# A fused attention and MLP kernel: the first chunk's q and k products made together, row tile by row tile, and the warm-up products fed from the program's constant zero

## The chip, the cores and the metric

The kernel runs on one core of one Trainium2 chip. The metric is device time in microseconds of one execution. Three runs of the kernel before took 414.65, 414.2 and 414.75 us; the median is 414.65. The profiled execution took 414.58 us, of which 412.7 us are the span from the first to the last instruction that the profile shows.

## The reference

For each token the result is a gated sum of an attention branch and an MLP branch, on the same input x of 2048 tokens by 448 features:

```python
g = sigmoid((x * gate_w).sum(-1, keepdims=True))
q, k, v = split(x @ wqkv)            # 16 heads of 28
# each token attends to itself and 7 earlier ones, 2 apart
logits = einsum("bhsd,bhswd->bhsw", q, k[idx]) * 28 ** -0.5   # masked where idx < 0
a = einsum("bhsw,bhswd->bhsd", softmax(logits), v[idx]) @ wo
b = relu(x @ w1 + b1) ** 2 @ w2 + b2  # 1792 hidden
out = g * a + (1 - g) * b
```

All inputs are float32. The change touches the first quarter of x @ wqkv alone.

## The kernel before

**Products in three parts.** Each float32 operand is split into a high part (rounded to the array's fp32r type by an ACT copy) and a low part (the rest, by a VectorE subtraction). A product of two operands is then three matrix products: high x high, high x low and low x high. In the names, `h` and `l` end the tiles: `wqh` and `wql` for the weights of q, k and v, `x.h` and `x.l` for the input.

**Tiling.** The 2048 tokens are four chunks of 512, each of four tiles of 128 tokens. The contraction has 448 rows: three row tiles of 128 (numbers 0 to 2) and a last one of 64, which is stored twice, on the lower and the upper 64 partitions (`w7h`, `w7l`, `x.x7`, `x.x8`). For each tile of tokens and each of q, k and v there is one PSUM accumulator (`Acc`) of 128 tokens by 448 columns (450 for q: two more columns carry the gate); it takes 3 x 3 full products and 3 on the last 64 rows. PSUM has eight accumulators, four under the tag `m` and four under `b`.

**Pairs.** TensorE can run two products on 64 rows side by side, one on the lower and one on the upper half of the array. `side_by_side` (L180) issues such pairs. A full product can also be made as two half products, one on each half, which must not be in flight on the same accumulator at once; `turn` (L191) stands between the halves: a tiny write to the accumulator by VectorE (or ACT), which waits for the first half and for which the second half waits.

**The first chunk, `qkv_first` (L257).** First, q of all four tiles (tag `b`), full products on 128 rows, row tile by row tile (L266): 12 products each, 36 in all. Then `run` works through a list of pairs: the last 64 rows of q beside those of k (12 pairs), then the 128-row products of k as half products (36 pairs), then v (42 pairs). v's four accumulators take the PSUM buffers of q.

**Evacuation, `qkv_evacuate` (L201).** ACT copies a finished accumulator to a staging tile `st` (L207) and, for q, the gate column to `zg` (L215). A staging tile holds two tiles of tokens; when the second is in, one DMA of 448 KB stores it to `q_d`, `k_d` or `v_d` (L213). There are `ST_BUFS = 3` staging buffers. In the first chunk q is evacuated as 0, 1, 2, 3, while the first pairs run, and k as 0, 2, 1, 3, later.

**The order of the work.** Nothing reorders instructions: each engine runs its own in program order, and waits by semaphores. Around the products a planner decides where in the program side work is issued. `advance` (L478) adds the planned time of the products just issued to a clock, and issues what `when` (L677) or `at` has set for an earlier time: the splits of v's weights at 12.0 us and 0.9 us apart, the spill of x to `x_d` at 10.5, the splits of the next chunk's x at 19.0 (`SPLIT_AT`, L682), the load of the chunk after at 23.5. `run` calls `advance` after each up to 12 pairs, then issues the step's turns, then its evacuations. All loads and stores go through SP's queue, one after the other.

**The start.** The program's constants are set by GpSimd ahead of a barrier (L1162). Then `WARM = 13` products of 128 x 256 on a tile of zeros (L632), which VectorE clears first (L629), keep TensorE busy until the first data is there. Meanwhile SP issues loads: for each row tile q's weights and x (L639, L644), then k's and v's weights (L649), the last 64 rows of v's (L652), and the next chunk's x (L565). The splits of q's weights and x follow (L654 to L667), and k's three after those (L711).

Of the kernel before, what the change touches and what calls it, by code (L numbers as in the profile page):

```python
# [7 lines left out]
F32 = mybir.dt.float32  # L8
F32R = mybir.dt.float32r
# [4 lines left out]
S, D, H, DH, W, F = 2048, 448, 16, 28, 8, 1792  # L14
P = 128
# [8 lines left out]
NQ = D + 2  # L24
# [7 lines left out]
MM448 = 203.0  # L32
# [15 lines left out]
LEAD = 5  # L48
DEFER = 2
ORDER = (3, 0, 1, 2)  # L50
WARM = 13
PP_BUFS = 4
ST_BUFS = 3
BT_BUFS = 8
# [3 lines left out]
def gated_mix_kernel(ctx: ExitStack, tc: tile.TileContext, xT, wqkv, w1, w2, wo, b1, b2, out):  # L58
    nc = tc.nc

    def f32(ap):
        return ap.bitcast(F32)
# [29 lines left out]
    attp = ctx.enter_context(tc.tile_pool(name="attp", bufs=1))  # L92
    smp = ctx.enter_context(tc.tile_pool(name="smp", bufs=2))
    prodp = ctx.enter_context(tc.tile_pool(name="prodp", bufs=1))
# [18 lines left out]
    def split_full(raw, hi, lo, soon=now):  # L113
        nc.scalar.activation(hi, raw, AF.Copy)
        soon(lambda: nc.vector.tensor_sub(lo, raw, f32(hi)))
# [29 lines left out]
    def ps(tag, name):  # L145
        return psum.tile([P, 512], F32, tag=tag, name=name, bufs=4)
# [6 lines left out]
    wqh = ap.tile([P, 3, NP + 2 * D], F32R, name="wqh")  # L153
    wql = ap.tile([P, 3, NP + 2 * D], F32R, name="wql")
# [10 lines left out]
    def ncols(b):  # L165
        return NQ if b == 0 else D

    def block(b):

        o = (0, NP, NP + D)[b]  # L170
        return slice(o, o + ncols(b))
# [8 lines left out]
    def side_by_side(*todo):  # L180


        assert len(todo[0]) == len(todo[1])
        for pair in zip(*todo):
            for r, (acc, a, w) in enumerate(pair):
                rows = slice(r * 64, r * 64 + 64)
                assert acc.rows in (None, r)
                nc.tensor.matmul(acc.pt[:, :acc.n], a[rows], w[rows], start=acc.todo == acc.all, stop=acc.todo == 1)  # L188
                acc.todo, acc.rows = acc.todo - 1, r

    def turn(one, two):  # L191


        for acc in (one, two) if one is not two else (one,):
            if one is two:
                nc.scalar.activation(acc.pt[0:1, 511:512], none, AF.Copy)
            else:
                nc.vector.memset(acc.pt[0:1, 511:512], 0.0)
            acc.rows = None
# [17 lines left out]
    def full(x, acc, tl, b, ks=range(3)):  # L217
        sl, n = slice(tl * P, tl * P + P), block(b)
        r = []
        for k in ks:  # L220
            r += [(acc, x.h[k][:, sl], wqh[:, k, n]), (acc, x.h[k][:, sl], wql[:, k, n]),
                  (acc, x.l[k][:, sl], wqh[:, k, n])]
        return r

    def last(x, acc, tl, b):

        sl = slice(tl * P, tl * P + P)
        n = block(1) if b == 2 else slice(0, ncols(b))
        h, l = w7h[:, n], w7l[:, n]
        return [(acc, x.x7[:, sl], h), (acc, x.x7[:, sl], l), (acc, x.x8[:, sl], h)]  # L230

    def accs(c, b, tls, tags):
        return [Acc(t, f"qkv{c}_{tl}_{b}", ncols(b)) for t, tl in zip(tags, tls)]

    def run(c, todo, steps):


        a = 0
        for e, done, *turns in steps:
            side_by_side(todo[0][a:e], todo[1][a:e])  # L240
            while a < e:
                n = min(12, e - a)
                if clock["on"] and a + n == e:

                    advance(max(n - LEAD, 0) * MM448)
                    while turns and not callable(turns[0]):
                        turn(*turns.pop(0))
                    n = min(n, LEAD)
                advance(n * MM448)
                a = min(a + 12, e)  # L250
            for t in turns:
                t() if callable(t) else turn(*t)
            for b, tl, acc in done:
                assert acc.todo == 0
                qkv_evacuate(acc.pt, c, tl, b)

    def qkv_first(x):  # L257


        four = range(4)  # L260
        q = accs(0, 0, four, "bbbb")
        for k in range(3):
            for two in ((0, 1), (2, 3)):
                for j, prods in enumerate(zip(*(full(x, q[i], i, 0, (k,)) for i in two))):
                    for acc, a, w in prods:
                        nc.tensor.matmul(acc.pt[:, :NQ], a, w, start=k == j == 0, stop=False)  # L266
            advance(12 * MM448)
        for acc in q:
            acc.todo = 3
        k = accs(0, 1, four, "mmmm")  # L270
        t = [sum((last(x, a[i], i, b) for i in four), []) for b, a in ((0, q), (1, k))]
        f = [full(x, k[i], i, 1) for i in four]
        run(0, [t[0] + f[0] + f[1] + f[2] + f[3], t[1] + f[2] + f[3] + f[0] + f[1]],
            [(3, [(0, 0, q[0])], (k[0], k[0])),
             (12, [(0, i, q[i]) for i in (1, 2, 3)], (k[1], k[1])),
             (24, [], (k[0], k[2])), (33, [], (k[1], k[3])),
             (39, [(1, 0, k[0]), (1, 2, k[2])]), (48, [(1, 1, k[1]), (1, 3, k[3])])])
        v = accs(0, 2, four, "bbbb")
        f, l = [full(x, v[i], i, 2) for i in four], [last(x, v[i], i, 2) for i in four]
        run(0, [f[0] + l[0] + f[2] + l[2] + f[1] + f[3], f[1] + l[1] + f[3] + l[3] + f[0] + f[2]],  # L280
            [(15, [], (v[0], v[1])), (24, [], (v[2], v[3])),
             (33, [(2, 0, v[0]), (2, 1, v[1])]), (42, [(2, 2, v[2]), (2, 3, v[3])])])
# [192 lines left out]
    def soon(fn):  # L475
        at(LO_DELAY, fn)

    def advance(dt):  # L478
        clock["pe"] += dt
        while due := [x for x in later if x[0] <= clock["pe"]]:  # L480
            item = min(due, key=lambda x: x[0])
            later.remove(item)
            item[1]()
        if not clock["on"]:
            clock["att"] = clock["pe"]
            return
        while clock["att"] < clock["pe"]:
            try:
                r = next(att)
            except StopIteration:  # L490
                clock["on"] = False
                return
            if r is None:
                clock["att"] = clock["pe"]
                return
            clock["att"] += r


    def raw_tile(name):
        return rawp.tile([P, 4, 512], F32, tag="raw", name=name)  # L500
# [124 lines left out]


    warm = ps("m", "warm")
    zero = prodp.tile([P, 2 * P], F32R, tag="pp", name="zero", bufs=PP_BUFS)
    nc.vector.memset(f32(zero), 0.0)  # L629
    nc.vector.memset(none, 0.0)  # L630
    for _ in range(WARM):
        nc.tensor.matmul(warm[:, :2 * P], zero[:, :P], zero, start=True, stop=True)  # L632


    raws = [raw_tile("wqraw0")]
    rx = raw_tile("xraw0")
    for k in range(4):
        if k < 3:
# [3 lines left out]
                nc.sync.dma_start(raws[0][rows, k, :NQ], wqkv[b, rows, k])  # L642
        for cols in ((slice(0, 256), slice(256, CH)) if k == 0 else (slice(0, CH),)):
            nc.sync.dma_start(rx[:, k, cols], xT[0, :, k, cols])  # L644

    for b, tag in ((1, "k"), (2, "v")):
        raw = attp.tile([P, 3, D], F32, tag=tag, name=f"wqraw{b}")
        for k in range(3):
            nc.sync.dma_start(raw[:, k], wqkv[b, :, k, :D])  # L649
        raws.append(raw)  # L650
    raw7 = attp.tile([P, D], F32, tag="q", name="wqraw7")
    nc.sync.dma_start(raw7, wqkv[2, :, 3, :D])  # L652
    x = x_tiles(0, xap)
    for k in range(3):  # L654
        nc.scalar.activation(wqh[:, k, :NQ], raws[0][:, k, :NQ], AF.Copy)
        halves = (slice(0, 256), slice(256, CH))
        for i, cols in enumerate(halves):

            if k == i == 0:
                nc.vector.tensor_copy(x.h[k][:, cols], rx[:, k, cols])  # L660
            else:
                nc.scalar.activation(x.h[k][:, cols], rx[:, k, cols], AF.Copy)
        nc.vector.tensor_sub(wql[:, k, :NQ], raws[0][:, k, :NQ], f32(wqh[:, k, :NQ]))
        for cols in halves:
            nc.vector.tensor_sub(x.l[k][:, cols], rx[:, k, cols], f32(x.h[k][:, cols]))
    split_full(raws[0][:, 3, :NQ], w7h[:, :NQ], w7l[:, :NQ])
    split_x78(rx[:, 3], x.x7, x.x8)  # L667

    def wq_split(b, k):
        if k < 3:  # L670
            split_full(raws[b][:, k], wqh[:, k, block(b)], wql[:, k, block(b)])
        else:
            split_full(raw7, w7h[:, NP:], w7l[:, NP:])
# [34 lines left out]
        nc.sync.dma_start(b1t, b1)  # L708
        nc.sync.dma_start(b2t, b2.partition_broadcast(P))

    for k in range(3):  # L711
        wq_split(1, k)
    for k in range(4):
        when(12000.0 + k * 900.0, wq_split, 2, k)
    for c, t in SPLIT_AT.items():
# [31 lines left out]
    for c in range(4):  # L747
        x = xs[c]
# [291 lines left out]
    c, x = ORDER[0], xm[3]  # L1040
# [8 lines left out]
    for g in range(2, 2 * NF):  # L1049
        i, f = g // (NF // 2), g % (NF // 2) * 2  # L1050
# [3 lines left out]
        last = g == 2 * NF - 1  # L1054
        if not f:
            x, slots = X([nxt[j][0] for j in range(4)]), [nxt[j][1] for j in range(4)]
            nxt = {}
        hold[0] = ends
        accs = h_first(x, c, f)
# [110 lines left out]
```

## Time and profile before

| | us |
|---|---|
| runs: 414.65, 414.2, 414.75; median | 414.65 |
| profiled execution, its own time | 414.58 |
| its span | 412.7 |
| TensorE busy | 408.4 (99%) |
| VectorE busy | 255.9 (62%) |
| ScalarE (ACT) busy | 211.9 (51%) |
| GpSimd (POOL) busy | 268.6 (65%) |
| warm-up products | from 1.20 to 4.13 |
| full products of q, first chunk | from 4.13 to 12.69 |

How to read the rows: the page gives busy time, share of the span and number of instructions of each engine. The chain that ended last, in order of time, has start, length, engine, tile, line and count. A row of the timeline has the start in us, the length in us, engine, line of the kernel, operation, written tile <- read tiles, shape and count; rows that follow each other closely with the same form are merged, and a bracket tells how long the engine sat idle before and what ended that. SPq rows are DMA issues, not transfers. A window row gives, for a stretch of time, the busy time of PE, PEld (weight load), DVE, ACT and POOL with instruction counts, then the granted TensorE clock, the busy share of the 16 DMA engines and GB/s. A DMA row gives the tiles, the number of issues, KB of each and the median time from issue to landing.

### The profile page before, as it was taken

Reading aid. Unit: us, or ns where it says so; the run is one execution under the profiler, and the core shown is the slowest. Engines: PE = TensorE matmul, PEld = TensorE weight load, DVE = VectorE, ACT = ScalarE, POOL = GpSimd, SP = SyncE. Lnnn points to the kernel's source line nnn. Section 1 sums busy time; section 2 is a strip of 40 time slices with the busy share of each in tenths; the row PEclk is TensorE's granted clock in tenths of the full one; section 3 lists DMA queues with packets and bytes.
Section 4 is the critical chain, followed back from the end, with each engine's and each line's share of the span. In section 5 each row is a group of like instructions: output and inputs, shape, how many; then the busy total and the mean of one; then the engine's idle time right before and its main releaser. Section 6 shows DMA issues by size and latency. Waiting matters only on the chain.

```text
span 412.7 us, 9323 instructions
## 1 busy us (share of the span) xinstructions
PE 408.4 (99%) x3835; PEld 377.6 (91%) x3835; DVE 255.9 (62%) x404; ACT 211.9 (51%) x477; POOL 268.6 (65%) x167
## 2 busy tenths in 40 slices
PE   8999999999999999999999999999999999999997
PEld 8999999999999999888888888989898888888996
DVE  4520523276767767777656798879576677892354
ACT  5642556378756565444565535444653254346540
POOL 0000000965989999999989899999899977860000
PEclk9999999999999999999999999999999999999999
DMA  7989799989164307654112649765145611168204
GB/s 236 380 318 326 227 364 292 363 259 321 47 224 159 128 2 258 207 186 152 37 50 93 233 157 266 200 149 149 24 163 192 224 46 59 72 175 139 91 0 180
DMA packets 65611, 73.76 MB, mean 179 GB/s; under 512 B 32352, under 2 KB 58528, under 8 KB 65184
## 3 DMA queue, kind: packets, MB, share of 16 engines
q1 hardware_dynamic: 65568, 73.16, 54.5%
q8 instruction: 30, 0.49, 0.5%
q14 instruction: 13, 0.11, 0.1%
HBM read 45.71 MB, written 28.25 MB: 179 GB/s over the span
## 4 chain that ended last, share of the span: by engine, by line
PE 99%; DVE 0%; issue 0%
PE b L188 33%; PE h L188 32%; PE qkv L188 23%; PE a L188 7%; PE qkv L266 2%; PE warm L632 1%; PE a L944 1%; PE last L944 0%; DVE bt L823 0%; PE last L936 0%; PE a L936 0%; DVE zero L629 0%; DVE b1z L630 0%
## 5 line engine op out<-in xcount | busy, mean ns | idle before, releaser
L339 POOL TENSOR_TENSOR qk<-q,k 128x896 f32<-128x896 f32 x64 | 135.0, 2138 | 83.2 <-DMA k<-k_d 78.9
L346 POOL TENSOR_TENSOR av<-lg,v 128x896 f32<-128x896 f32 x64 | 119.5, 1962 | 8.0 <-DVE lg L340 5.6
L188 PE MATMUL qkv<-wqh,x 64*128 64x448 f32 (+1 forms) x528 | 90.9, 360 | 0.0
L619 DVE TENSOR_TENSOR h<-h,h 128x512 fp32r<-128x512 f32 x56 | 38.3, 687 | 60.8 <-ACT h L622 60.4
L188 PEld LDWEIGHTS qkv<-wqh,x 64*128 64x128 f32 x528 | 74.0, 184 | 1.3
L188 PE MATMUL qkv<-wql,x 64*128 64x448 f32 (+1 forms) x264 | 74.7, 360 | 0.0
L188 PE MATMUL b<-w2ah,h 64*128 64x448 f32 x448 | 70.4, 359 | 0.0
L188 PE MATMUL b<-w2bh,h 64*128 64x448 f32 x448 | 69.6, 360 | 0.0
L340 DVE TENSOR_REDUCE lg<-qk 128x32 f32<-128x896 f32 x64 | 67.1, 1076 | 2.2 <-POOL qk L339 2.1
L354 DVE TENSOR_REDUCE o<-av 128x112 f32<-128x896 f32 x64 | 66.5, 1070 | 2.1 <-POOL av L346 1.8
L620 ACT ACTIVATE h<-h,b1z 128x512 f32<-128x512 f32 x56 | 36.7, 656 | 44.0 <-PE h L188 44.0
L188 PEld LDWEIGHTS b<-w2ah,h 64*128 64x128 f32 x448 | 48.0, 184 | 2.8
L188 PEld LDWEIGHTS b<-w2bh,h 64*128 64x128 f32 x448 | 46.0, 184 | 3.2 <-ACT h L571 0.3
L188 PE MATMUL b<-w2al,h 64*128 64x448 f32 x224 | 47.6, 358 | 0.0
L188 PEld LDWEIGHTS qkv<-wql,x 64*128 64x128 f32 x264 | 45.5, 184 | 0.7
L188 PE MATMUL b<-w2bl,h 64*128 64x448 f32 x224 | 45.8, 358 | 0.0
L207 ACT ACTIVATE st<-qkv 128x448 f32<-128x448 f32 x48 | 24.5, 543 | 32.2 <-PE qkv L188 27.1
L188 PE MATMUL h<-x,w1h 64*128 64x512 f32 x168 | 36.1, 386 | 0.0
L621 ACT ACTIVATE h<-h 128x512 fp32r<-128x512 f32 x56 | 33.5, 599 | 1.7
L622 ACT ACTIVATE h<-h 128x512 f32<-128x512 f32 x56 | 33.2, 593 | 0.0
L188 PE MATMUL h<-x,w1l 64*128 64x512 f32 x84 | 29.7, 386 | 0.0
L571 ACT ACTIVATE h<-h 128x4 fp32r<-128x4 f32 (+1 forms) x35 | 7.2, 206 | 42.6 <-PE b L188 42.4
(145 smaller groups left out, 749.4 us busy)
## 6 DMA issues: line engine op xcount, KB each, us to landing
k<-k_d SPq DMA_DIRECT2D x8, 840.0 KB, 6.7
v<-v_d SPq DMA_DIRECT2D x8, 840.0 KB, 4.4
x_d<-x SPq DMA_DIRECT2D x11, 512.0 KB, 6.0
q_d<-st SPq DMA_DIRECT2D x8, 448.0 KB, 4.6
k_d<-st SPq DMA_DIRECT2D x8, 448.0 KB, 4.1
v_d<-st SPq DMA_DIRECT2D x8, 448.0 KB, 7.1
w1raw<-w SPq DMA_DIRECT2D x4, 896.0 KB, 10.0
q<-q_d SPq DMA_DIRECT2D x8, 448.0 KB, 3.6
```

What stands on the lines that cost most here:

```text
L188: nc.tensor.matmul(acc.pt[:, :acc.n], a[rows], w[rows], start=acc.todo == acc.all, stop=acc.todo == 1)
L207: nc.scalar.activation(st[:, :, t % 2], pt[:, :D].rearrange("p (g c) -> p g c", g=G), AF.Copy)
L266: nc.tensor.matmul(acc.pt[:, :NQ], a, w, start=k == j == 0, stop=False)
L339: nc.gpsimd.tensor_mul(pr, q[:, s:s + 1].to_broadcast([P, W, C]), k[:, s:s + W])
L340: pending.append(lambda: nc.vector.tensor_reduce(lg[:, s], pr.rearrange("p w (h d) -> p w h d", h=HG), axis=AX.X, op=ALU.add))
L346: nc.gpsimd.tensor_mul(pr.rearrange("p (h d) w -> p w h d", h=HG), lg[:, s][:, :, :, None].to_broadcast([P, W, HG, DH]), v[:, s:s + W].rea ...
L354: nc.vector.tensor_reduce(o[:, g * C:(g + 1) * C], pr, axis=AX.X, op=ALU.add)
L571: nc.scalar.activation(ap, f32(ap), AF.Copy)
L619: nc.vector.tensor_sub(hl, pt, f32(hh))
L620: ops += [lambda pt=pt, r=r: nc.scalar.activation(pt, pt, AF.Relu, bias=b1t[:, f + r:f + r + 1]), lambda pt=pt, hh=hh: nc.scalar.activatio ...
L621: lambda pt=pt, hh=hh: nc.scalar.activation(hh, pt, AF.Square),
L622: lambda pt=pt, r=r, low=low: (nc.scalar.activation(pt, pt, AF.Square), at(delays[r], low))]
```

## The change

It has three parts.

1. The warm-up products read the program's constant zero, one element a partition, repeated, instead of a tile that VectorE clears. There are 15 of them instead of 13.
2. `qkv_first` opens the accumulators of q (tag `b`) and of k (tag `m`) together. For each of the three row tiles it issues 12 full products of q and then 12 of k. The pairs on the last 64 rows, q beside k, follow; after each three pairs one tile of q and the same tile of k are evacuated. k's half products and their turns are gone.
3. The loads of k's weights move up: one behind q's weights and x in each row tile. Their splits move up in the same way, to the end of each row tile's splits.

By the planner's clock 36 more products come before the pairs, so that the splits of v's weights and the spill of x, which keep their due times, now stand before the evacuations of q instead of behind them.

```diff
-WARM = 13
+WARM = 15
...
-        q = accs(0, 0, four, "bbbb")
-        for k in range(3):
-            for two in ((0, 1), (2, 3)):
-                for j, prods in enumerate(zip(*(full(x, q[i], i, 0, (k,)) for i in two))):
-                    for acc, a, w in prods:
-                        nc.tensor.matmul(acc.pt[:, :NQ], a, w, start=k == j == 0, stop=False)
-            advance(12 * MM448)
-        for acc in q:
+        q, k = accs(0, 0, four, "bbbb"), accs(0, 1, four, "mmmm")
+        for r in range(3):
+            for b, tiles in ((0, q), (1, k)):
+                for two in ((0, 1), (2, 3)):
+                    for j, prods in enumerate(zip(*(full(x, tiles[i], i, b, (r,)) for i in two))):
+                        for acc, a, w in prods:
+                            nc.tensor.matmul(acc.pt[:, :acc.n], a, w, start=r == j == 0, stop=False)
+                advance(12 * MM448)
+        for acc in q + k:
             acc.todo = 3
-        k = accs(0, 1, four, "mmmm")
-        t = [sum((last(x, a[i], i, b) for i in four), []) for b, a in ((0, q), (1, k))]
-        f = [full(x, k[i], i, 1) for i in four]
-        run(0, [t[0] + f[0] + f[1] + f[2] + f[3], t[1] + f[2] + f[3] + f[0] + f[1]],
-            [(3, [(0, 0, q[0])], (k[0], k[0])),
-             (12, [(0, i, q[i]) for i in (1, 2, 3)], (k[1], k[1])),
-             (24, [], (k[0], k[2])), (33, [], (k[1], k[3])),
-             (39, [(1, 0, k[0]), (1, 2, k[2])]), (48, [(1, 1, k[1]), (1, 3, k[3])])])
+        run(0, [sum((last(x, tiles[i], i, b) for i in four), []) for b, tiles in ((0, q), (1, k))],
+            [(3 * i + 3, [(0, i, q[i]), (1, i, k[i])]) for i in four])
...
-    zero = prodp.tile([P, 2 * P], F32R, tag="pp", name="zero", bufs=PP_BUFS)
-    nc.vector.memset(f32(zero), 0.0)
+    zero = nc.const_aps.tensor(0.0, [P, 2 * P], F32).bitcast(F32R)
...
+    for b, tag in ((1, "k"), (2, "v")):
+        raws.append(attp.tile([P, 3, D], F32, tag=tag, name=f"wqraw{b}"))
...
-    for b, tag in ((1, "k"), (2, "v")):
-        raw = attp.tile([P, 3, D], F32, tag=tag, name=f"wqraw{b}")
-        for k in range(3):
-            nc.sync.dma_start(raw[:, k], wqkv[b, :, k, :D])
-        raws.append(raw)
+        if k < 3:
+            nc.sync.dma_start(raws[1][:, k], wqkv[1, :, k, :D])
+    for k in range(3):
+        nc.sync.dma_start(raws[2][:, k], wqkv[2, :, k, :D])
...
         for cols in halves:
             nc.vector.tensor_sub(x.l[k][:, cols], rx[:, k, cols], f32(x.h[k][:, cols]))
+        split_full(raws[1][:, k], wqh[:, k, block(1)], wql[:, k, block(1)])
...
-    for k in range(3):
-        wq_split(1, k)
```

## The prediction, made before the changed kernel was run

> **What bounds the kernel now.** I read the page's totals first, then the chain that ended last in order of time, then the timeline of the first 32 us on all engines, then the DMA views.
>
> ```profile
> span 412.7 us, 9323 instructions
> PE 408.4 (99%) x3835; PEld 377.6 (91%) x3835; DVE 255.9 (62%) x404; ACT 211.9 (51%) x477; POOL 268.6 (65%) x167
> ...
> PE 99%; DVE 0%; issue 0%
> ```
> ```profile
> 1.20 3.14 PE warm L632 x13
> 4.33 8.42 PE qkv L266 x36
> 12.76 92.19 PE qkv L188 x894
> ```
>
> TensorE is the chain from 1.20 us on: the pieces join without a gap, through the first chunk and on to 105 us. So no wait of TensorE is there to be removed by a reordering, and any wait that is added goes into the end time in full. The first 13 us show what else there is to win.
>
> ```profile
> 0.24 0.10 POOL L1162 MEMSET const-float32-0.0<- 128x1 f32 x1 [0.24 <-issue]
> ...
> 0.74 1.28 ACT L655 ACT_TABLE_LOAD   x1 [0.74 <-PEq L1162]
> ...
> 0.87 0.27 DVE L629 MEMSET zero<- 128x256 f32 x1 [0.87 <-PEq L1162]
> ...
> 1.20 3.14 PE L632 MATMUL warm<-zero 128*128 128x256 f32 x13 [1.20 <-DVE b1z L630]
> ...
> 3.64 0.29 DVE L660 CAST x<-xraw 128x256 fp32r<-128x256 f32 x1 [2.50 <-DMA xraw<-xT]
> ...
> 4.13 1.03 PE L266 MATMUL qkv<-wqh,x 128*128 128x450 f32 x2
> ...
> 4.96 0.95 PE L266 MATMUL qkv<-wql,x 128*128 128x450 f32 x2
> ...
> 5.54 0.42 ACT L662 ACTIVATE x<-xraw 128x256 fp32r<-128x256 f32 x1 [1.63 <-DMA xraw<-xT]
> 5.71 1.44 PE L266 MATMUL qkv<-wqh,x 128*128 128x450 f32 x4
> ...
> 7.39 0.96 PE L266 MATMUL qkv<-wqh,x 128*128 128x450 f32 x4
> ...
> 8.20 0.56 PE L266 MATMUL qkv<-wql,x 128*128 128x450 f32 x2
> ...
> 12.69 0.47 PE L188 MATMUL qkv<-w7h,x 64*128 64x450 f32 x2
> ...
> 13.00 0.37 PE L188 MATMUL qkv<-w7l,x 64*128 64x448 f32 x2
> ...
> 15.01 0.42 PE L188 MATMUL qkv<-w7h,x 64*128 64x448 f32 x2
> ```
>
> Two products take 0.75 us (4.96 to 5.71), four take 0.81 later (7.39 to 8.20): the pace goes from 0.375 to 0.2 us between 5.7 and 7.4. The first products run at half pace though the granted clock column says 1.00 throughout. A pair of half-row products takes 0.2 too: ten pairs from 13.00 to 15.01. Only a mode's first pair takes 0.31 (12.69 to 13.00).
>
> **Warm-up.** It waits for the two VectorE memsets (0.87 and after) and starts at 1.20; the program's zero is written at 0.24, ahead of the barrier. Engines leave that barrier between 0.74 (ACT) and 0.87 (DVE): I take 0.80 as TensorE's start. Thirteen took 4.13 - 1.20 = 2.93, so 0.225 each; fifteen end at 0.80 + 3.38 = 4.18 against 4.13, 0.05 late. The data is ready at 3.93 (3.64 + 0.29), so warm-up still sets the start. A delay in the half-pace stretch displaces slow products, so it costs 0.05 x 0.2/0.375 = 0.03. Bounds: start at 0.74, -0.01; no earlier than 1.20, 0.45 x 0.53 = +0.24. If the end of the half pace moves ahead with the start, by 0.4 us, that saves 0.4 x (1 - 0.53) = 0.19; if it does not, nothing: I take -0.10.
>
> The Trainium skill, page TensorE: Matmul & The Clock Gate, section Part 1, says that the array's clock is halved until one whole free-running window of about 3.4 us was busy. The trace agrees with a late release: some 5 us of products ran before the pace changed. By that rule the release moves by a whole window or not at all in one execution: the -0.10 would be 0 or the -0.55 of a rival below, and the sum +1.63 or +1.08.
>
> **Order of the products.** 36 half-row pairs of k become 36 full products, 0.2 us each either way: nothing. Both need 0.31 for one change of mode. The work ahead of T, the start of the first pair on the last 64 contraction rows, grows by 36 x 0.2 = 7.2: T goes from 12.69 to 19.9. The two ACT turns and four VectorE turns of k vanish; the chain had no wait on them: nothing.
>
> **Loads and splits moved up.**
>
> ```profile
> 23.55 2.19 ACT L114 ACTIVATE x<-xraw 128x512 fp32r<-128x512 f32 x4
> ...
> 24.21 1.93 DVE L115 TENSOR_TENSOR x<-xraw,x 128x512 fp32r<-128x512 f32 x3 [4.40 <-ACT x L114]
> ...
> 25.50 0.06 DVE L198 MEMSET qkv<- 1x1 f32 x2
> ```
>
> ```profile
> 5.00:6.00 1.00, 1.00 (x4) 0.91 (x3) 0.01 (x1) 0.42 (x1) 0.00 (x0) 1.00 0.94 316
> ```
> ```profile
> 10.00:15.00 5.00, 5.00 (x36) 4.49 (x36) 2.95 (x6) 3.82 (x12) 0.00 (x0) 1.00 1.07 400
> ```
> ```profile
> 10.93 0.33 SPq L565 DMA_DIRECT2D xraw<-xT  x1
> ```
> ```profile
> xraw<-xT SPq DMA_DIRECT2D x1, 1024.0 KB, 5.8
> ```
>
> The first rows are splits: 0.55 us each on ACT, 0.64 on VectorE. The two rows of windows end in DMA share and GB/s: the queues are full through these stretches. The last two are the issue of the next chunk's x and its time to land, 10.93 + 5.8 = 16.7.
>
> Three loads of k's weights (448 columns) go ahead on SP's queue. With them row tiles 1 and 2 of q and x are later by some 0.7 and 1.4 us (0.23 MB each at 316 GB/s), and three ACT and three VectorE splits stand between q's. But row tile 1 is now needed at product 25 instead of 13, 2.4 us later, and row tile 2 is needed 4.8 later. The k tile 0 splits stand where q's tile 1 splits did and are needed at the same product, 13. All cost nothing, as long as loads arrive in issue order. v's splits, ordered behind q's evacuations before, now stand ahead of them, four of 0.55 us in the 5 us or so before T in which ACT has nothing else: nothing.
>
> **Evacuations.** This is where I find the cost.
>
> ```profile
> 13.64 0.16 ACT L196 ACTIVATE qkv<-b1z 1x1 f32<-1x1 f32 x1 [1.15 <-PE qkv L188]
> 13.75 0.52 ACT L207 ACTIVATE st<-qkv 128x448 f32<-128x448 f32 x1
> 14.17 0.14 ACT L215 ACTIVATE zg<-qkv 128x1 f32<-128x1 f32 x1
> ...
> 14.37 0.52 ACT L207 ACTIVATE st<-qkv 128x448 f32<-128x448 f32 x1
> ...
> 14.84 0.55 ACT L207 ACTIVATE st<-qkv 128x448 f32<-128x448 f32 x1
> ...
> 14.91 1.49 SPq L213 DMA_DIRECT2D q_d<-st  x2
> ...
> 20.88 0.98 ACT L207 ACTIVATE st<-qkv 128x448 f32<-128x448 f32 x2 [2.95 <-PE qkv L188]
> ```
>
> The evacuations now run q0 k0 q1 k1 q2 k2 q3 k3, and the pool of staging tiles has three buffers, each for two row tiles. q0/q1 take the first, k0/k1 the second, q2/q3 the third; k2 needs the first again, and must wait until the store of q0/q1 has landed. The built program has that wait on k2's evacuation, and q3 stands behind it on ACT. v3's accumulator is the PSUM buffer of q3: TensorE's first product of v3 waits for q3's evacuation.
>
> In times from T: q0 starts at 0.95 (13.64 - 12.69). A q takes 0.47 (14.37 to 14.84), a k 0.44 (0.98 for two less 0.54 for the last). So k0 1.42, q1 1.86, k1 2.33, q2 2.77; k2 could start at 3.24. q1's copy ends at 1.86 + 0.52 = 2.38, and its store is issued at 2.40 (before: 14.89, 14.91). How long it takes to land:
>
> ```profile
> 30.34 0.36 SPq L213 DMA_DIRECT2D v_d<-st  x1
> ```
> ```profile
> 30.50:31.00 0.50, 0.50 (x8) 0.50 (x6) 0.00 (x0) 0.00 (x0) 0.00 (x0) 1.00 0.00 0
> 31.00:31.50 0.50, 0.50 (x9) 0.50 (x7) 0.00 (x0) 0.37 (x1) 0.00 (x0) 1.00 0.52 165
> 31.50:32.00 0.50, 0.50 (x8) 0.50 (x6) 0.00 (x0) 0.50 (x2) 0.00 (x0) 1.00 0.98 330
> ```
> ```profile
> DMA to landing us min/median/max: 2.8/3.7/9.4
> ```
> ```profile
> q_d<-st SPq DMA_DIRECT2D x2, 448.0 KB, 4.5
> ```
>
> The windows follow a store issued to queues that had run empty: no byte until after 31.0, then 448 KB at some 335 GB/s, 1.4 us. The landing row is that of all transfers with q_d: 2.8 least. The q_d row is of the two stores issued at 14.91, which queued behind x's load: 4.5. In the new order the spill of x (four 512 KB transfers) goes ahead of the stores on SP; behind the load that lands at 16.7 its 2.1 MB take 5.2 us at 400 GB/s, to 21.9. The store is issued at 19.9 + 2.4 = 22.3, so the queues should be empty. I take 3.0, near the least, with 2.8 and 4.5 as ends.
>
> It lands at 5.40, k2 starts at 5.45, q3 at 5.89, its gate column ends at 5.89 + 0.42 + 0.14 = 6.45, and TensorE goes on at 6.51. It wants v0 and v1 at 0.31 + 11 x 0.2 = 2.51 (q1 is out at 2.42: no wait) and v2 and v3 12 pairs later, at 4.91. The stall is 1.60 us; ends 1.40 and 3.10.
>
> Behind it, ACT's splits of the next x come late too, and VectorE's turn of v0 and v1 stands behind two of their subtractions, as it does before (the rows from 23.55). k3 at 6.36, splits from 6.80, the turn 1.95 later (23.55 to 25.50) and done by 8.81; TensorE asks for it at 6.51 + 2.40 = 8.91. Just in time: nothing, up to 0.2 if handoffs are slower. SP's queue holds the next x load behind k's second store: some 3 us later than 24.2, but its landing was far ahead of its use. The rest of the kernel shifts as a whole.
>
> **Sum.** +0.03 - 0.10 + 1.60 = +1.53. Against the profiled execution's 414.58 (span 412.70 and 1.88 around it) that is 416.11, span 414.2. The median of the runs shown, 414.65, stands 0.07 above it: 416.2.
>
> **Rivals.** Late landing: the spill's tail or a slow ring is still ahead of the store, and it lands in 3.7 to 4.5: stall 2.3 to 3.1, 416.9 to 417.7. For it speaks the 3.7 median, against it the 22 us estimate.
>
> Half pace again: if TensorE's idle 1.6 us brings the slow pace back, for 1 to 5.4 us (as long as it lasted from 1.20 to some 6.6), that costs 0.47 of it, 0.5 to 2.5 more; with 1.5, 417.7. No row shows a gap of that size in mid-stream. The Trainium skill, same page, section Why this matters for your kernels, puts the danger at gaps over about 3 us, which would exclude it; no run here shows it.
>
> A release one step earlier: if the earlier start ends the half pace before 4 us, products 1 to 6 run at 0.2, and product 7 then waits for the second half of x, split by 5.96 (5.54 + 0.42), instead of starting near 6.46. The gain is bounded at 0.55; with the stall and the 0.03 +1.08: 415.7. No row tells which it will be. This is the case that the Trainium skill's window rule (Part 1, above) allows.
>
> Not slower: the wait on the staging buffer is hidden. It decides at one place: if q0/q1's store lands by T + 3.82 (4.91 less 1.09 from k2's start to TensorE), 1.4 us after issue, v3 finds its buffer free. Then only the warm-up terms are left, -0.07 to -0.52: 414.1 to 414.6. Against it: 0.66 us or more passes before the first byte (30.34 to 31.0), and 1.4 for the bytes. It also holds the case that a buffer is free for another reason.
>
> **How the numbers follow.** Stall near 1.6: 0.63. Late landing: 0.14. Half pace again: 0.05. Earlier release with the stall: 0.08, of which 0.02 falls within 0.2% (0.83 us, about what a measurement of this kernel can tell from no change). Wait hidden: 0.10, with 0.03 for faster by over 0.2% and 0.07 within. Slower is 0.63 + 0.14 + 0.05 + 0.06 = 0.88, same 0.09, faster 0.03. The likeliest case alone, with landings from 2.8 to 3.4 and the release term from 0 to -0.19, gives 415.9 to 416.7. The range goes on to the earlier release below and to landings of 4.3 above, and leaves out the hidden wait and the latest ones: 415.3 to 417.5.
>
> **What would show it.** One gap of TensorE of about 1.6 us near 25 us, ended by ACT's copy of q3; k2's copy waiting on the DMA of q_d; the warm-up starting near 0.8; no other gap from 4.2 to 25. Wrong would be a k2 that starts at 3.2 after T, a second gap at the turn, or a gap among the first 24 products.

## The result, and the profile after

The changed kernel took 419.93 us (median; 417.76 to 421.13) against 414.7 us for the kernel before in the same comparison: a ratio of 1.0117, with a 95% interval of 1.009 to 1.0144. It is slower, as forecast, but by 5.2 us instead of 1.5, and above the range. The profiled execution is the longest of the six: 421.13 us, span 419.0.

The page of the changed kernel first: its span, the busy times, and the shares of the chain that ended last.

```profile
span 419.0 us, 9245 instructions
...
PE 411.2 (98%) x3801; PEld 379.9 (91%) x3801; DVE 254.9 (61%) x399; ACT 211.6 (51%) x475; POOL 268.3 (64%) x167
...
PE 96%; DMA 2%; ACT 1%; SPq 0%; DVE 0%; issue 0%; ACTq 0%
```

The chain is no longer TensorE alone: DMA and ACT have entered it. In order of time it reads so (start, length, what):

```profile
6.16 13.82 PE qkv L267 x66
19.98 0.84 PE qkv L188 x6
20.82 0.53 ACT st L207
...
21.42 0.88 ACT st L207 x2
...
22.32 5.20 DMA q_d<-st
...
27.62 0.98 ACT st L207 x2
...
28.72 31.37 PE qkv L188 x278
```

From 20 to 28.7 us the chain leaves TensorE: copies of q0, k0 and q1 on ACT, the store of q0/q1, then k2's and q3's copies, then TensorE again. The store holds 5.20 us of it. The timeline of the same execution shows what TensorE saw; the bracket gives how long the engine sat idle and what ended that.

```profile
0.78 3.46 PE L626 MATMUL warm<-const-float32-0.0 128*128 128x256 f32 x15 [0.78 <-PEq L1156]
...
4.12 0.65 PE L267 MATMUL qkv<-wqh,x 128*128 128x450 f32 x2
...
4.66 0.68 PE L267 MATMUL qkv<-wql,x 128*128 128x450 f32 x2
...
6.16 0.67 PE L267 MATMUL qkv<-wqh,x 128*128 128x450 f32 x2 [0.41 <-ACT x L657]
...
19.91 0.47 PE L188 MATMUL qkv<-w7h,x 64*128 64x450 f32 x2
...
20.81 0.55 ACT L207 ACTIVATE st<-qkv 128x448 f32<-128x448 f32 x1 [5.13 <-PE qkv L188]
...
22.32 0.38 SPq L213 DMA_DIRECT2D q_d<-st  x1
...
24.82 0.36 PE L188 MATMUL qkv<-wqh,x 64*128 64x448 f32 x1
27.62 0.98 ACT L207 ACTIVATE st<-qkv 128x448 f32<-128x448 f32 x2 [4.33 <-DMA q_d<-st]
...
28.72 0.74 PE L188 MATMUL qkv<-wqh,x 64*128 64x448 f32 x1 [3.54 <-ACT zg L215]
```

v2's first half product starts at 24.82, its partner v3 at 28.72. Without a wait they start together, so the stop is worth 28.72 - 24.82 = 3.9 us less the 0.2 of that pair's turn: 3.7. Then there is a second loss. The windows of the stretch that follows end in granted clock, DMA share and GB/s:

```profile
27.00:28.00 1.00, 0.00 (x0) 0.00 (x0) 0.00 (x0) 0.38 (x1) 0.00 (x0) 0.96 0.17 56
28.00:34.00 6.00, 5.28 (x28) 4.76 (x30) 2.66 (x8) 3.17 (x8) 0.00 (x0) 0.50 0.77 243
34.00:35.00 1.00, 1.00 (x8) 0.91 (x8) 0.00 (x0) 0.00 (x0) 0.00 (x0) 0.62 1.00 426
```

The granted clock falls to half just before 28 (0.96 of that microsecond) and is back at 34.8 (0.62 of that one): 6.8 us, of which TensorE worked 6.0 at half pace and lost about 2.8 (0.47 of it, by the paces of 0.375 and 0.2 us). So 3.7 + 2.8 = 6.5 us is lost between 24.8 and 34.8 us. That accounts, within 0.2 us, for a span that is 419.0 - 412.7 = 6.3 us longer; the rest of this execution's 421.13 - 414.58 = 6.55 us lies outside the span.

Of the other executions only the span and the mean clock are known, and these fit in the main. The one with a granted clock of 1.000 over its span took 417.76, four with 0.996 took 419.73 to 420.68, the profiled one with 0.992 took 421.13. A deficit of 0.004 of 418 us is 1.7 us of clock, 3.4 us at half rate: by this figure those four had half as long a slow stretch as the profiled one. The clock does not explain everything: 417.76 is only 3.1 us above the kernel before, so the stop in that execution should have been shorter than 3.7, and 417.76 + 1.7 = 419.5 is still 0.3 to 1.2 below the four. That the stops differ in length is likely, and no trace shows it.

### The profile page after: what moved, and what is told of

The parts are those of the page before. It is cut to its first block, busy times and chain, and to the rows that moved or that the text cites. A ratio compares the mean times of both kernels' runs of the same rounds, so it can differ in the third digit from the quotient of the medians.

```text
span 419.0 us, 9245 instructions
## 1 busy us (share of the span) xinstructions
PE 411.2 (98%) x3801; PEld 379.9 (91%) x3801; DVE 254.9 (61%) x399; ACT 211.6 (51%) x475; POOL 268.3 (64%) x167
## 4 chain that ended last, share of the span: by engine, by line
PE 96%; DMA 2%; ACT 1%; SPq 0%; DVE 0%; issue 0%; ACTq 0%
PE b L188 32%; PE h L188 32%; PE qkv L188 21%; PE a L188 7%; PE qkv L267 3%; DMA q_d<-st 1%; DMA xraw<-xT 1%; PE a L938 1%; ACT st L207 1%; PE last L938 0%; DVE bt L817 0%; ACT x L657 0%; SPq L641 0%; SPq L636 0%; PE last L930 0%
## 5 line engine op out<-in xcount | busy, mean ns | idle before, releaser
L188 PE MATMUL qkv<-wqh,x 64*128 64x448 f32 (+1 forms) x480 | 84.0, 368 | 3.5 <-ACT zg L215 3.5
L188 PEld LDWEIGHTS qkv<-wqh,x 64*128 64x128 f32 x480 | 63.7, 190 | 4.8 <-ACT zg L215 3.9
L188 PE MATMUL b<-w2ah,h 64*128 64x448 f32 x448 | 67.7, 359 | 0.0
L188 PE MATMUL qkv<-wql,x 64*128 64x448 f32 (+1 forms) x240 | 60.3, 368 | 0.0
L188 PEld LDWEIGHTS b<-w2ah,h 64*128 64x128 f32 x448 | 44.3, 184 | 2.8
L188 PE MATMUL b<-w2al,h 64*128 64x448 f32 x224 | 42.2, 358 | 0.0
L188 PE MATMUL b<-w2bl,h 64*128 64x448 f32 x224 | 41.8, 358 | 0.0
L188 PEld LDWEIGHTS qkv<-wql,x 64*128 64x128 f32 x240 | 36.0, 190 | 0.5
L188 PE MATMUL h<-x,w1h 64*128 64x512 f32 x168 | 31.6, 386 | 0.0
L188 PE MATMUL h<-x1b,w1h 64*128 64x512 f32 x168 | 28.1, 386 | 0.0
```

## The experiments

**A fourth staging buffer.** k2 and k3 of the first chunk are staged in a buffer of another pool, so that nothing waits for the store.

```diff
+        if first and (c, tl, b) == (0, 2, 1):
+            stage[b, t // 2] = prodp.tile([P, G, 2, C], F32, tag="pp", name="st_k23", bufs=PP_BUFS)
-        if first:
+        elif first:
```

> The changed kernel, but k2's and k3's staging tile of the first chunk comes from another pool, as a fourth buffer, so that k2's copy waits for no store. Theory (the wait for the staging buffer stops ACT, ACT stops v3, and the half pace that follows comes from that stop alone): TensorE's gap of 3.7 us near 25 us and the half pace behind it both vanish, the granted clock is 1.00, and the time is the kernel before less what the warm-up saves, 414.2 to 414.7. Rival (the new order itself costs the time: loads and splits moved up, or k's products on all 128 rows): the time stays near 420, with the loss in other places than the gap.

Measured: 415.26 us, ratio 1.0023 (1.0014 to 1.0032). The gap near 25 us is gone and so is the slow stretch, as this window shows:

```profile
24.00:36.00 12.00, 12.00 (x123) 11.95 (x121) 2.74 (x12) 4.68 (x11) 0.00 (x0) 1.00 1.05 365
```

Over the kernel before in its own comparison (414.46) 0.8 us are left of 5.2, so this one wait was worth about 4.4. The rest of the order of products and loads is as in the changed kernel, so the rival that the order itself costs the time is out, but for the 0.8 us that the theory did not have. In the profiled execution (415.07 us) 0.4 us of them are at 50 us. Rows of the timeline of this kernel, and one of its chain:

```profile
46.56 0.55 ACT L209 ACTIVATE st<-qkv 128x448 f32<-128x448 f32 x1 [4.36 <-DMA v_d<-st]
...
50.60 0.06 DVE L198 MEMSET qkv<- 1x1 f32 x2
```
```profile
37.45 9.01 DMA v_d<-st
```

A copy of the second chunk waits 4.36 us for a store of v, and behind it VectorE's turn is late; TensorE stops for 0.4 us at 50.1 in the profiled execution. In the kernel before, that copy stood at 43.84, and the same store, issued at 36.75, took 7.0 us:

```profile
v_d<-st SPq DMA_DIRECT2D x1, 448.0 KB, 7.0
```

So the transfers are late. Why they are is tested by the last of the experiments.

**The spill behind the stores.** The staging wait stays, but the spill of x is set later.

```diff
-    when(10500.0, x_spill, 0, x)
+    when(18500.0, x_spill, 0, x)
```

> The changed kernel, but the spill of the first x is set for 18.5 us on the planner's clock instead of 10.5, so that SP issues it behind the four stores of q and k. The staging wait stays. Theory (the store of q0/q1 took 5.2 us to land, and not 3.0, because 2.1 MB of spill were still ahead of it): it lands in about 3 us, the stop of TensorE is 1.6 us instead of 3.7, too short for the half pace to come back, and the time is about 416.2. Rival (the landing takes 5 us by itself, since these stores are made of short pieces): no change, a stop of 3.5 to 4 us, near 420.

Measured: 420.71 us, ratio 1.0152 (1.0138 to 1.0166). The time is not the one expected, but the stop near 25 us is. The DMA view from 22 to 27 us, and the rows of ACT for k2 and q3 and of TensorE for v3:

```profile
q_d<-st SPq DMA_DIRECT2D x2, 448.0 KB, 2.8
```
```profile
25.32 0.98 ACT L207 ACTIVATE st<-qkv 128x448 f32<-128x448 f32 x2 [1.97 <-DMA q_d<-st]
...
26.41 0.47 PE L188 MATMUL qkv<-wqh,x 64*128 64x448 f32 x1 [1.18 <-ACT zg L215]
```

With the queues empty the store lands in 2.8 us instead of 5.2, ACT waits 1.97 instead of 4.33, TensorE stops for about 1.3 us (v2 starts at 24.87, v3 at 26.41, less 0.2), and the granted clock stays up there. That is the stop which the prediction had. But the 2.1 MB are now ahead of later transfers: the chain near 50 us begins with one store of v.

```profile
40.63 11.04 DMA v_d<-st
...
51.78 0.55 ACT st L207
...
52.38 7.81 PE qkv L188 x49
```

It takes 11.04 us to land (7.0 in the kernel before, and 9.0 with the fourth buffer, where the spill is in its old place), the same wait for a staging buffer holds ACT, TensorE stops for 2.8 us at 49.4, and half pace follows from 53.8 to 57.2, by the clock of these windows (0.50 between them):

```profile
53.00:54.00 1.00, 1.00 (x13) 0.99 (x11) 1.00 (x2) 1.00 (x3) 0.00 (x0) 0.88 0.00 0
...
57.00:58.00 1.00, 1.00 (x12) 0.94 (x10) 0.56 (x4) 0.00 (x0) 0.00 (x0) 0.91 0.99 279
```

This is the profiled execution (421.28 us, clock 0.995). One of the four kept a clock of 1.000 and still took 420.45; what it lost instead is open. In the kernel before, the queues are full from 32 to 44 us too (a DMA share of 0.99), so that there is little room for a transfer that moves:

```profile
32.00:44.00 12.00, 12.00 (x122) 11.95 (x120) 1.60 (x8) 2.85 (x9) 0.00 (x0) 1.00 0.99 331
```

**Short fillers.** TensorE gets 30 products into unused columns of v2's accumulator, ahead of the first pair of v2 and v3, while it waits.

```diff
+FILL = 30
...
+            if filler[0] and a <= 12 < e:
+                pt, w, h = filler[0]
...
+                for _ in range(FILL):
+                    nc.tensor.matmul(pt[:, 450:512], h[:, :P], w[:, 0, :62], start=True, stop=True)
```

> The changed kernel with 30 products of 128 x 62 into unused columns of v2's accumulator, issued by TensorE just ahead of the wait for q3's evacuation; their results are used by nothing. Theory (the stop costs about 3.5 us, and the half pace that follows another 1.6 to 2.9 because TensorE sat idle): TensorE stops as before, but has work for most of it; the half pace does not come back, the granted clock is 1.00 in all runs, and the time is about 417.9. Rival (the half pace has another cause, such as a fixed time after the start): near 420 with the same slow stretch, or above it by the length of the fillers.

Measured: 419.71 us, ratio 1.0124 (1.0109 to 1.0139). Inconclusive: two executions of four kept the clock (span 416.7 and 417.0), two did not (418.2, clock 0.995 and 0.996), and of these two there is no trace. In the profiled one the fillers cover the stop:

```profile
25.32 3.54 PE L248 MATMUL qkv<-wqh,x 128*128 128x62 f32 x30
```

But they start 0.118 us apart (3.54 / 30) with 62 columns each, where the products of q bring 450 columns in 0.2.

**Full fillers.** The same with 17 products of 448 columns, which v2's own first product overwrites.

```diff
-FILL = 30
+FILL = 17
-                    nc.tensor.matmul(pt[:, 450:512], h[:, :P], w[:, 0, :62], start=True, stop=True)
+                    nc.tensor.matmul(pt[:, :448], h[:, :P], w[:, 0, :448], start=True, stop=True)
```

> The changed kernel with 17 products of 128 x 448 into v2's accumulator while TensorE waits for q3's evacuation; v2's own first product overwrites them, so that nothing uses their results. The fillers of 62 columns kept the clock at 1.00 in two of four runs, and the other two were 1.2 us longer. Theory (short products leave the array mostly idle; full ones keep it busy): no half pace in any run, and the stop alone is left, 3.5 to 3.9 us over the kernel before: 418.0 to 418.6. Rival (the half pace has another cause than the idle array): runs at 419.5 to 421 as without fillers.

Measured: 418.95 us, ratio 1.0099 (1.0084 to 1.0115); all four executions lie between 418.85 and 419.07, with a clock of 0.999 or 1.000. Two windows of this kernel, and the same two of the changed kernel:

```profile
24.00:29.00 5.00, 5.00 (x33) 4.20 (x31) 0.00 (x0) 1.77 (x5) 0.00 (x0) 1.00 0.53 183
29.00:36.00 7.00, 7.00 (x71) 6.52 (x72) 2.60 (x8) 3.51 (x8) 0.00 (x0) 1.00 0.95 312
```
```profile
24.00:29.00 5.00, 1.46 (x14) 1.09 (x13) 0.00 (x0) 1.38 (x5) 0.00 (x0) 0.89 0.61 215
29.00:36.00 7.00, 7.00 (x44) 6.34 (x46) 2.66 (x8) 2.17 (x5) 0.00 (x0) 0.59 0.83 281
```

From 29 to 36 us TensorE gets 71 products done instead of 44, at a clock of 1.00 instead of 0.59. With full products in the stop the clock stays up in four executions of four, without them it fell in five of six: the idle array is what brings the half pace back. What is left is the stop alone, 4.0 us over the kernel before in its own comparison. That is 0.1 more than the 3.5 to 3.9 expected, and the fillers end after the wait (q3's store is issued at 28.23 in the profiled execution, v2 starts at 28.88). Its spread is 0.2 us, against 3.4 of the changed kernel. Part of that kernel's spread is thus the half pace; but the fillers also give the stop a fixed length, so that an earlier or later landing would not show here, and the shares of the two are open.

**k's third row tile later.** Its load and split go behind those of the last 64 rows.

```diff
-        if k < 3:
+        if k < 2:
             nc.sync.dma_start(raws[1][:, k], wqkv[1, :, k, :D])
+    nc.sync.dma_start(raws[1][:, 2], wqkv[1, :, 2, :D])
...
+        if k < 2:
             split_full(raws[1][:, k], wqh[:, k, block(1)], wql[:, k, block(1)])
     split_full(raws[0][:, 3, :NQ], w7h[:, :NQ], w7l[:, :NQ])
     split_x78(rx[:, 3], x.x7, x.x8)
+    split_full(raws[1][:, 2], wqh[:, 2, block(1)], wql[:, 2, block(1)])
```

> The changed kernel, with the load and the split of k's third row tile put behind those of the last 64 rows. The split of the last 64 rows ends earlier, and the load of the next x, which needs the buffer that this split reads, is issued about 1.2 us earlier (12.4 instead of 13.65), and with it the spill and the store behind it. Theory (the store lands late because the next x's load was issued late and everything behind it in the queues moved): the store lands about 4.1 us after its issue instead of 5.2, TensorE stops for 2.6 us instead of 3.7, and the half pace comes back in fewer executions: about 417.5, and down to 417.0 where it does not. Rival (the place of this load does not matter): like the changed kernel, 419.9.

Measured: 419.52 us, ratio 1.011 (1.0089 to 1.0132). In the changed kernel the next x's load is issued at 13.65, right behind VectorE's split of the last 64 rows, and the queues run below full until its bytes come (162 and 254 GB/s, against 400 from 10 to 15 us before the change):

```profile
13.00 0.63 DVE L115 TENSOR_TENSOR w7l<-wqraw,w7h 128x450 fp32r<-128x450 f32 x1 [0.32 <-ACT w7h L114]
...
13.65 0.33 SPq L560 DMA_DIRECT2D xraw<-xT  x1
```
```profile
14.00:15.00 1.00, 1.00 (x7) 0.94 (x6) 1.00 (x3) 1.00 (x3) 0.00 (x0) 1.00 0.44 162
15.00:20.00 5.00, 5.00 (x27) 4.38 (x25) 1.37 (x3) 0.68 (x2) 0.00 (x0) 1.00 0.87 254
```
```profile
x_d<-x SPq DMA_DIRECT2D x4, 512.0 KB, 8.9
xraw<-xT SPq DMA_DIRECT2D x1, 1024.0 KB, 6.7
```

Now it is issued at 12.88, 0.8 earlier rather than 1.2, and the store lands 0.9 sooner:

```profile
12.88 0.33 SPq L560 DMA_DIRECT2D xraw<-xT  x1
```
```profile
q_d<-st SPq DMA_DIRECT2D x1, 448.0 KB, 4.3
```

TensorE stops for 2.8 us instead of 3.7 (v2 starts at 25.05, v3 at 28.04, less 0.2), and the clock falls again:

```profile
28.04 0.54 PE L188 MATMUL qkv<-wqh,x 64*128 64x448 f32 x1 [2.63 <-ACT zg L215]
```
```profile
28.00:32.00 4.00, 3.96 (x24) 3.55 (x26) 2.54 (x6) 2.49 (x5) 0.00 (x0) 0.57 0.88 256
```

The mechanism holds; the time does not follow, because in the profiled execution (420.6 us) a stop of 2.8 us still brings the half pace. Two more executions have a clock of 0.996 (419.06 and 419.98), one kept 0.999 (418.17); how long their stops were is on no trace.

**q first, then k.** The order of the evacuations alone.

```diff
-            [(3 * i + 3, [(0, i, q[i]), (1, i, k[i])]) for i in four])
+            [(3 * i + 3, [(0, i, q[i])]) for i in range(3)]
+            + [(12, [(0, 3, q[3])] + [(1, i, k[i]) for i in four])])
```

> The changed kernel, but q is evacuated as 0, 1, 2, 3 and k after it, so that no q stands behind the wait for the staging buffer. Theory (ACT is what is held up, and everything behind k2 on ACT is late): v3 starts on time, but the next x's splits wait behind k2, and VectorE's turn of v0 and v1 behind two of them, so that TensorE stops for about 3 us one step later, near 27 us: 418 to 420. Rival (only the accumulators of q matter): the gap goes, 414.3 to 415.3.

Measured: 420.11 us, ratio 1.0133 (1.0113 to 1.0152). Rows of its timeline:

```profile
27.48 0.37 PE L188 MATMUL qkv<-w7h,x 64*128 64x448 f32 x2
27.86 0.98 ACT L207 ACTIVATE st<-qkv 128x448 f32<-128x448 f32 x2 [3.30 <-DMA q_d<-st]
...
30.67 0.06 DVE L198 MEMSET qkv<- 1x1 f32 x2
30.81 0.47 PE L188 MATMUL qkv<-wqh,x 64*128 64x448 f32 x2 [2.96 <-DVE qkv L198]
```

v3 starts on time, and TensorE stops one step later for 3.1 us, at VectorE's turn, which stands behind splits that wait for copies that ACT makes after k2. The half pace follows here too: the clock is 0.992 to 0.995 in all four executions. A wait on an engine that works in order holds all that stands behind it, whichever instruction is put next.

**The warm-up alone.** The kernel before with 15 products on the constant zero.

```diff
-WARM = 13
+WARM = 15
-    zero = prodp.tile([P, 2 * P], F32R, tag="pp", name="zero", bufs=PP_BUFS)
-    nc.vector.memset(f32(zero), 0.0)
+    zero = nc.const_aps.tensor(0.0, [P, 2 * P], F32).bitcast(F32R)
```

> The kernel before with the new warm-up alone: 15 products on the constant zero, started without VectorE. Theory (the warm-up starts at 0.78 instead of 1.20, q starts at the same time, and the half pace ends earlier by 0.4 us on average): 0.0 to 0.3 us less than before, 414.4 to 414.7. Rival (reading one repeated element makes the products slower or the warm-up collides with the loads): 0.2 us or more above before.

Measured: 414.4 us against 414.46, ratio 0.9999 (0.999 to 1.0008). No difference: this part neither costs nor saves what these runs can tell.

**Fourth buffer and later third row tile together.** The diffs of both, as above.

> The fourth staging buffer and the later load and split of k's third row tile together. With the fourth buffer alone the time was 415.26, with a gap of 0.4 us near 50 us that ends with a turn of VectorE, behind a copy of ACT that waits for a store of v. Theory (this gap comes from the transfers that are late since the next x's load was issued late): it shrinks or goes, and the time is 414.3 to 414.9. Rival (it comes from the new order of the stores and splits itself): 415.2 as before.

Measured: 414.66 us, ratio 1.0001 (0.9992 to 1.0009). The chain of this kernel in order of time has TensorE from 6.36 to 60 us in two pieces that join:

```profile
6.36 13.63 PE qkv L269 x66
20.00 40.03 PE qkv L188 x386
```

No gap is left at 25 or at 50 us. The store of v that took 9.0 us with the fourth buffer alone takes 7.6 here, and 7.0 in the kernel before. The two runs differ by the place of k's third row tile alone, and their intervals (1.0014 to 1.0032, and 0.9992 to 1.0009) do not overlap: the 0.8 us came from that place. With the wait gone and the next x's load earlier, the new order costs nothing and gains nothing. No version tried here beats the kernel before.

## Why the prediction was wrong

The direction, the place and the mechanism of the stop were right: k2's copy waits for the staging buffer, and q3 and so v3 stand behind it. What failed is how long the store takes to land, and then what a longer stop does to the clock. Of the prediction's signs of being wrong one came, a gap among the first 24 products: 0.4 us ahead of 6.16, which its rival with the earlier release had. Point by point:

- **Warm-up.** Start 0.80 forecast, 0.78 measured; q at 4.18 forecast, 4.12 measured. In the profiled execution the half pace ended near 4.1, the case of the rival with the earlier release. The products then waited for the second half of x (split from 5.69 on, product at 6.16), as that rival said. But its gain, up to 0.55, did not last: 0.15 went at 8.02, where a product waited for the low split of k's first row tile (done at 7.95), and T came at 19.91 against 19.9. Alone the part is within noise (0.9999, 0.999 to 1.0008); the sum had -0.07 for it.
- **Order of the products: nothing.** Right: with the fourth buffer and the later third row tile the new order takes as long as the kernel before.
- **Loads and splits moved up: nothing.** Wrong, and the root of the late landing below. The prediction asked whether q's and k's data come in time, not what stands behind them. The splits of k pushed back the split of the last 64 rows of q's weights, and with it the next x's load. Even without the staging wait this cost 0.8 us (the fourth buffer alone).
- **When the store is issued.** 22.3 forecast, 22.32 measured. ACT's steps up to there were right to 0.1 us.
- **How long it takes to land: the step that failed first.** 3.0 was taken, with 4.5 as the end; it took 5.20. The reason given was that behind "the load that lands at 16.7" the spill would be done at 21.9. But that load waits for the split of the last 64 rows of q's weights (it reuses the buffer they were read from), and the change itself, by the loads and splits of k, moves that split back. So the load was issued 2.7 us later than before (13.65 against 10.93), it took 6.7 us instead of 5.8 to land, and the spill was still ahead of the store: the spill's transfers took 8.9 us. With the spill out of the way the store takes 2.8, the least end of the prediction. The prediction counts a stop up to v3's start: so counted it is 1.5 there, against 1.40 for that end, and 3.9 in the changed kernel (3.7 by the count above) against 1.60. The 2.2 us by which the landing was taken too short are nearly all of the difference. So the handoffs were right, and the term was mis-sized by what is in the queue. (The 1.09 us from k2's start to TensorE is 1.06 by the prediction's own times; nothing hangs on it.)
- **Half pace again, at 0.05: the second failure.** It was priced at 1.5 and came in five of six executions, at some 1.7 in four (by their mean clock) and 2.8 in the profiled one. The chance was tied to a stop of 1.6 us. In the profiled executions a stop of 1.3 us did not bring it, and stops of 2.8, 3.1 and 3.7 us did. So, as far as these lengths tell, it hung on the first error. The Trainium skill, page TensorE: Matmul & The Clock Gate, section Why this matters for your kernels, warns of gaps over about 3 us; here TensorE's idle gap of 2.63 us (at 28.04, with k's third row tile later) was enough, so the measurement decides for a smaller limit in this kernel.
- **The range.** It treated the late landing and the half pace as separate cases, and stopped at a landing of 4.3. They come together, since the half pace came with the longer stops: put together after the fact, 3.7 + 1.7 - 0.1 gives 419.95 from 414.65, where 419.93 was measured. That it is so near is in part luck, as the stops of the other executions are not known and the -0.1 is not measured.

## What to carry to other kernels

Before costing a store at its empty-queue time, follow the load ahead of it to what releases its buffer: a split that is moved by a microsecond moves a megabyte, and everything behind it in one queue. When two products are evacuated in turns, count the staging buffers in the new order, and look at what stands behind the first copy that must wait; a copy that is put in its place only moves the stop. And a stop of TensorE has two prices: its length, and from a length on that lay between 1.3 and 2.8 us here, the slow stretch that follows.

## What the runs showed of the hardware

- The half pace comes and goes in steps. By the granted clock it lasted 6.8 us in the profiled execution of the changed kernel (27.9 to 34.8), and 3.4 us in three other traces: the spill behind the stores (53.8 to 57.2), k's third row tile later (28.3 to 31.7), q first (31.9 to 35.3). It need not begin within the stop: in the first of these three TensorE had been at work again since 52.38. The Trainium skill, page TensorE: Matmul & The Clock Gate, section Part 1, tells of windows of about 3.4 us; the two lengths fit one and two of them.
- With 62-column products 0.118 us apart in the stop the clock was kept in two executions of four, with 448-column products at 0.2 us in four of four. Short products thus seem not to count in full; where the other two executions lost the clock is on no trace.
- The column of the granted clock reads 1.00 in the first microseconds, where products ran at half pace. At the start of a span the pace of the products tells more than that column.
- A transfer that is moved out of one queue's way is in the way later: 2.1 MB of spill, put behind the stores instead of ahead of them, took 2.4 us off one landing (5.2 to 2.8), and another, issued 18 us later, took 11.0 instead of the 9.0 that it took with the fourth buffer and the spill in its place.
